# Gate products in float32 column quarters, in a kernel of attention, an MLP and a routed expert layer

## The chip, the cores and the metric

One core of one Trainium2 chip runs the whole program. The metric is the device time of one execution in microseconds. The engines are named as in the profile: PE is TensorE's matmul, PEld its weight load, DVE is VectorE, ACT is ScalarE, POOL is GpSimd, SP is SyncE, from whose queue nearly all DMAs are issued.

## The reference, cut to what matters

```python
# attention: q, k, v are 4 x 12 x 448 x 64; rows of q and k are normalized, softmax, product with v
x = attn.transpose(0, 2, 1, 3).reshape(1792, 768)
# MLP
h = x @ w_in                                # 768 x 2048
g = h * np.clip(h + 3.0, 0.0, 6.0) / 6.0
x = g @ w_out                               # 2048 x 768
# experts
logits = x @ w_gate                         # 768 x 8
# greedy assignment over all logits in falling order, at most 224 tokens per expert
# each token's expert: relu(x @ w1[e]) @ w2[e], 768 -> 1024 -> 768
```

The weights w_in and w_out may come as 64-bit floats, and the kernel first narrows them to float32.

## The kernel before, in words

A float32 product is made of three products in fp32r: each operand is split into a high part (a copy to fp32r, on ACT) and a low part (the rest, on DVE or POOL), and high x high, high x low and low x high are summed in PSUM. Some products with few columns (L371, L420 and L429 in the attention) are plain float32 products instead.

The program runs in this order. First the attention, two heads at a time, for four batches of 448 tokens. An order written out by hand (events with due times, and a queue of small pieces, "atoms", that `fill` draws from) sets every engine's order here. Between the attention of batch b the first MLP layer (L520) of batch b - 1 runs: for each of 16 units f of 128 hidden columns it does 18 products of 128 x 128 by 128 x 448, then ACT and DVE make g, and g goes to DRAM (g_dr). Then comes the first layer for batch 3, with nothing of the attention beside it. Then the second layer (L1135): 14 tiles of 128 tokens, by 16 f, by three products, by two column parts. The high and low parts g2h and g2l of g are read back from DRAM. Routing runs inside the second layer, a step after a given count of its products; it starts when the queue of leftover atoms is empty. The experts follow. From the first layer of batch 3 on only TensorE's order is written out; the other engines' orders, SP's DMA queue among them, come from a planner that lays them out by estimated times.

The logits are not taken from the second layer's result. They are computed as g @ (w_out @ w_gate), so that routing can run while the second layer does. Two parts serve that:

- `wprime_atoms` makes w_out @ w_gate in the attention of batch 3, merged into the first layer of batch 2. In 48 steps (8 pairs of units f, 6 chunks of 128 columns of w_out) it transposes two blocks (L659), splits the result into a high part (ACT, L661) and a low part (DVE, L662), and two steps later multiplies both with the gate's weights (L670, L671, L673; 8 or 16 stationary columns, 256 moving). The high and low products lie beside each other in 16 rows and are transposed back and added (L681 to L684); wp is the result, split again.
- `lg(b, f)` multiplies unit f of wp with unit f of g of batch b: two products of 448 columns (L570 and L571, or L573). `gsplit` makes the parts gh (ACT, L557) and gl (DVE, L558). For batch 3 this is done inline, two units behind the first layer. For batches 0 and 1, `late_lg_atoms` reads g back from DRAM into gr (L611, four buffers) and the atoms are merged into the first layer of batch 3. For batch 2 and the last two units of batch 3 the atoms are drawn from the queue in the second layer, one for every seven products. `lg_end` copies the 16 rows of a batch, transposes them in blocks of 128 tokens (L599) and adds high and low part into L, which routing reads.

In the first layer of batch 3 there also are the loads and splits of w_in (L178, L115, L116) and of w_out (L814, L115, L116).

Of the kernel before, what the change touches and what calls it, by code (L numbers as in the profile page):

```python
# [8 lines left out]
F32 = mybir.dt.float32  # L9
# [4 lines left out]
OP = mybir.AluOpType  # L14
# [7 lines left out]
def kernel(  # L22
# [82 lines left out]

    half = const.tile([128, 1], F32, name="half")
    nc.vector.memset(half, 0.5)
    wp = const.tile([128, NF, 16], F32R, name="wp")
    L = const.tile([128, NTC, E], F32, name="L")


# [382 lines left out]
    def mlp1_atoms(b, inline):  # L494
# [16 lines left out]
        def mm(f, n):  # L511
            if n == 0:
                unit_start(f)
            c, t = divmod(n, 3)
            wh, wl, w = state["w"]
            xh, xl = XT[b]
            lhs = (wh, wh, wl)[t]
            x = (xh, xl, xh)[t]
            p = state["ps"]
            nc.tensor.matmul(p[:, :S], lhs[:, c], x[:, c], start=(n == 0), stop=(n == 3 * NC - 1))  # L520
            if n == 3 * NC - 1:
                r = mpool.tile([128, S], F32, name="r", bufs=1)
                nc.scalar.activation(r, p[:, :S], AF.Relu, bias=half, scale=1.0 / 6.0)
                g = mpool.tile([128, S], F32, name="g", bufs=GB)
                nc.vector.scalar_tensor_tensor(g, r, 1.0, p[:, :S], op0=OP.min, op1=OP.mult)
                state["g", f] = g
                if inline:
                    gsplit(b, f, g, nc.vector)

        def g_out(f):  # L530
            nc.sync.dma_start(g_dr[b][f * 128:(f + 1) * 128, :], state.pop(("g", f)))
# [1 line left out]
        for f in range(NF):  # L533
            for n in range(3 * NC):
                atoms.append(lambda f=f, n=n: mm(f, n))
                if n == GD and f > 0:
                    atoms.append(lambda f=f: g_out(f - 1))
                if n == WD2 and b in whole_b:
                    atoms.append(prefetch)
                if inline and n == 10 and f > 1:  # L540
                    atoms.append(lambda f=f: lg(b, f - 2))
        atoms.append(lambda: g_out(NF - 1))
        if inline:
            for f in (NF - 2, NF - 1):
                late.append(lambda f=f: lg(b, f))
            late.append(lambda: lg_end(b, 0))
            late.append(lambda: lg_end(b, 1))
        return atoms
# [1 line left out]
    GS = {}  # L550
    LGM = {}

    def gsplit(b, f, g, eng):
        k, n = (1, GI) if b == B - 1 else (0, GL)
        gh = tpool[0].tile([128, S], F32R, name=f"gh{k}", bufs=n)
        gl = tpool[0].tile([128, S], F32R, name=f"gl{k}", bufs=n)
        nc.scalar.activation(gh, g, AF.Copy)  # L557
        eng.tensor_tensor(gl, g, gh.bitcast(F32), op=OP.subtract)  # L558
        GS[b, f] = (gh, gl)

    def lg(b, f):
        if f == 0:
            if b < B - 1:
                lgp[b] = ps.tile([128, 512], F32, name="lg", tag="b", bufs=8)
            else:
                lgp[b] = ps.tile([128, 512], F32, name="lg", tag="b", bufs=8)
        p = lgp[b]
        gh, gl = GS.pop((b, f))
        if f > 0:
            nc.tensor.matmul(p[:8, :S], wp[:, f, 0:8], gl, start=False, stop=False, skip_group_check=True)  # L570
        nc.tensor.matmul(p[:16, :S], wp[:, f, :], gh, start=(f == 0), stop=(f == NF - 1))  # L571
        if f == 0:
            nc.tensor.matmul(p[:8, :S], wp[:, f, 0:8], gl, start=False, stop=False, skip_group_check=True)  # L573

    def lg_end(b, part):

        p, odd = lgp[b], b % 2
        if part == 0:
            s = tpool[0].tile([16, S], F32, name="lgs", bufs=1)
            nc.vector.tensor_copy(s, p[:16, :S])  # L580
            if b // 2 not in LGM:
                LGM[b // 2] = [tpool[0].tile([16, 128], F32, name="lgm", bufs=2), 0]
            m = LGM[b // 2]
            m[1] += 1
            nc.scalar.activation(m[0][:, odd * 64:odd * 64 + 64], p[:16, 0:64] if odd else p[:16, S - 64:S], AF.Copy)
            lgp[b] = s
            return
        m, n = LGM[b // 2]
        s = p[:, odd * 64:odd * 64 + 384]
        src = [s[:, k * 128:(k + 1) * 128] for k in range(3)]  # L590
        c0 = 4 if odd else 0
        if n == 2:
            src = [m] + src if odd else src + [m]
# [2 lines left out]
        n = len(src)  # L596
        t = ps.tile([128, 512], F32, name="t", tag="b", bufs=8)
        for c, x in enumerate(src):
            nc.tensor.transpose(t[:, 16 * c:16 * c + 16], x, ident[:16, :16])  # L599
        s2 = tpool[0].tile([128, 4, 16], F32, name="lgs2", bufs=1)  # L600
        nc.scalar.activation(s2[:, :n], t[:, :16 * n].rearrange("p (c e) -> p c e", e=16), AF.Copy)
        c0 += 7 * (b // 2)
        nc.vector.tensor_tensor(L[:, c0:c0 + n, :], s2[:, :n, 0:8], s2[:, :n, 8:16], op=OP.add)

    def late_lg_atoms(bs):

        GR = {}

        def ld(b, f):
            GR[b, f] = tpool[0].tile([128, S], F32, name="gr", bufs=4)  # L610
            nc.sync.dma_start(GR[b, f], g_dr[b][f * 128:(f + 1) * 128, :])  # L611

        todo = [(b, f) for b in bs for f in range(NF)]
        atoms = []
        n = len(todo)
        for i in range(n + 4):
            def one(i=i):
                if i < n:
                    ld(*todo[i])
                if 1 < i < n + 2:  # L620
                    b, f = todo[i - 2]
                    gsplit(b, f, GR.pop((b, f)), nc.vector)
                if i > 3:
                    b, f = todo[i - 4]
                    if f == 1 and b != bs[0]:
                        lg_end(b - 1, 1)
                    lg(b, f)
                    if f == NF - 1:
                        lg_end(b, 0)
            atoms.append(one)  # L630
        atoms.append(lambda: lg_end(bs[-1], 1))
        return atoms


    def wprime_atoms():
        wg = apool.tile([128, NC, E], F32, name="wg", bufs=1)
        nc.sync.dma_start(wg, w_gate.rearrange("(c p) e -> p c e", p=128))
        wgs = apool.tile([128, NC, 16], F32R, name="wgs", bufs=1)
        nc.scalar.activation(wgs[:, :, 0:8], wg, AF.Copy)
        nc.vector.tensor_tensor(wgs[:, :, 8:16], wg, wgs[:, :, 0:8].bitcast(F32), op=OP.subtract)  # L640
        wsum = apool.tile([128, NF, E], F32, name="wsum", bufs=1)
        T3 = 3
        tt = apool.tile([128, T3, 2, 256], F32R, name="wo_t", bufs=1)
        raws, st = {}, {}

        def ld(f):
            raws[f] = stage("wo_v")
# [5 lines left out]
        def one(g, c):  # L653
# [6 lines left out]
            o = tt[:, (g * NC + c) % T3]  # L660
# [3 lines left out]
        def two(g, c):  # L664
            if c == 0:
                st["acc"] = ps.tile([128, 512], F32, name="lg", tag="b", bufs=8)
            p = st["acc"]
            o = tt[:, (g * NC + c) % T3]
            if c > 0:
                nc.tensor.matmul(p[:8, :256], wgs[:, c, 0:8], o[:, 1], start=False, stop=False, skip_group_check=True)  # L670
            nc.tensor.matmul(p[:16, :256], wgs[:, c], o[:, 0], start=(c == 0), stop=(c == NC - 1))  # L671
            if c == 0:
                nc.tensor.matmul(p[:8, :256], wgs[:, c, 0:8], o[:, 1], start=False, stop=False, skip_group_check=True)  # L673
            if c == NC - 1:
                st["s", g] = apool.tile([16, 256], F32, name="wps", bufs=2)
                nc.scalar.activation(st["s", g], p[:16, :256], AF.Copy)

        def three(g):
            t = ps.tile([128, 512], F32, name="h", tag="b", bufs=8)
            for k in range(2):  # L680
                nc.tensor.transpose(t[:, 16 * k:16 * k + 16], st["s", g][:, k * 128:(k + 1) * 128], ident[:16, :16])  # L681
            v = apool.tile([128, 2, 16], F32, name="wpv", bufs=2)
            nc.scalar.activation(v, t[:, :32].rearrange("p (f e) -> p f e", e=16), AF.Copy)
            nc.vector.tensor_tensor(wsum[:, 2 * g:2 * g + 2], v[:, :, 0:8], v[:, :, 8:16], op=OP.add)  # L684
            if g == NF // 2 - 1:
                nc.scalar.activation(wp[:, :, 0:8], wsum, AF.Copy)
                nc.vector.tensor_tensor(wp[:, :, 8:16], wsum, wp[:, :, 0:8].bitcast(F32), op=OP.subtract)

        todo = [(g, c) for g in range(NF // 2) for c in range(NC)]
        atoms = []  # L690
        for i in range(len(todo) + 4):
            def step(i=i):
                if i < len(todo):
                    one(*todo[i])
                if 1 < i < len(todo) + 2:
                    two(*todo[i - 2])
# [634 lines left out]
```

## Time and profile before

| | us |
|---|---|
| median of 3 runs | 1215.1 (1214.14 to 1218.32) |
| profiled execution | 1219.53 |
| its span | 1217.7 |
| TensorE busy | 1145.3 |
| VectorE busy | 780.7 |
| ScalarE busy | 552.1 |
| GpSimd busy | 490.6 |

The profile is of one execution. Its span runs from the first to the last instruction; all times in the rows below count from the span's start. Matmuls overlap in their pipeline, so the duration of one (0.36 us for 448 columns in fp32r) is longer than the distance from one start to the next. The mean granted TensorE clock is 0.978 of full speed.

### The profile page before, as it was taken

The numbers are of one execution on the slowest core, as the hardware profiler recorded it, in microseconds if no ns is written. First come the engines' busy times: TensorE is split into PE (matmuls) and PEld (weight loads), VectorE is DVE, ScalarE is ACT, GpSimd is POOL, SyncE is SP. The second block draws the span as 40 slices with busy tenths as digits, with TensorE's granted clock in tenths as the row PEclk, the third lists the DMA queues.
The fourth block names the chain that finished last, engine by engine and source line by source line (L and its number), as shares of the span: only waits on it lengthen the run. The fifth ranks groups of instructions, "written<-read, shape, count | busy, mean of one in ns | idle before, by whom it ended". The sixth has DMA issues, their size and how long they took to land.

```text
span 1217.7 us, 19761 instructions
## 1 busy us (share of the span) xinstructions
PE 1145.3 (94%) x7204; PEld 931.2 (76%) x7204; DVE 780.7 (64%) x1580; ACT 552.1 (45%) x1019; POOL 490.6 (40%) x362
## 2 busy tenths in 40 slices
PE   3988999999999999999979999999998799999997
PEld 2877656667676677787758787777778799999997
DVE  7887977767657665346893466666676675555550
ACT  3655646555454555446663111111123566555650
POOL 2222554754345432112352222222243677666640
PEclk9888999999999999999999999999999899999999
DMA  4355998977786866649895222222234688778731
GB/s 127 116 163 144 261 303 255 302 273 242 236 279 214 277 223 241 211 149 321 261 298 157 61 75 66 79 57 65 79 100 129 203 257 263 229 235 240 230 116 45
DMA packets 210708, 230.84 MB, mean 190 GB/s; under 512 B 24338, under 2 KB 183732, under 8 KB 210612
## 3 DMA queue, kind: packets, MB, share of 16 engines
q1 hardware_dynamic: 207284, 218.58, 58.3%
q0 software_dynamic: 3328, 11.01, 3.0%
q8 instruction: 56, 0.92, 0.3%
q14 instruction: 40, 0.33, 0.1%
HBM read 178.57 MB, written 50.98 MB: 189 GB/s over the span
## 4 chain that ended last, share of the span: by engine, by line
PE 62%; DVE 14%; DMA 9%; issue 6%; ACT 4%; POOL 2%; SPq 1%; POOLq 0%; DVEq 0%; ACTq 0%
PE y L1135 16%; PE h L520 10%; PE y L1283 8%; PE h L1219 5%; PE st L331 4%; PE av L420 3%; PE av L371 3%; PE h L1221 2%; PE sm L429 2%; PE rt L945 2%; DMA gr<-g_dr 1%; DMA wo_s<-wo 1%; PE s L309 1%; DVE C L940 1%; DMA we_s<-in_moe_w_dram 1%
## 5 line engine op out<-in xcount | busy, mean ns | idle before, releaser
L520 PE MATMUL h<-xh,w 128*128 128x448 f32 x768 | 240.3, 381 | 0.6 <-DVE mr L320 0.3
L520 PEld LDWEIGHTS h<-xh,w 128*128 128x128 f32 x768 | 144.8, 192 | 30.6 <-issue 14.3
L1078 POOL TENSOR_TENSOR g2l<-gr,g2h 128x512 fp32r<-128x512 f32 x60 | 79.1, 1319 | 207.1 <-ACT g2h L1076 159.8
L520 PE MATMUL h<-xl,w 128*128 128x448 f32 x384 | 145.7, 379 | 0.0
L312 DVE TENSOR_REDUCE mx<-s 112x1 f32<-112x448 f32 x192 | 105.9, 612 | 54.2 <-PE s L309 54.1
L1076 ACT ACTIVATE g2h<-gr 128x512 fp32r<-128x512 f32 x60 | 37.9, 631 | 207.1 <-PE y L1135 157.5
L1135 PE MATMUL y<-woh,g2l 128*128 128x512 f32 (+1 forms) x448 | 128.7, 349 | 1.0 <-POOL g2l L1078 1.0
L1135 PE MATMUL y<-woh,g2h 128*128 128x512 f32 (+1 forms) x448 | 128.1, 349 | 0.0
L1135 PE MATMUL y<-wol,g2h 128*128 128x512 f32 (+1 forms) x448 | 126.4, 346 | 0.0
L116 DVE TENSOR_TENSOR wel<-we_s,weh 128x768 fp32r<-128x768 f32 x59 | 80.6, 1372 | 61.5 <-ACT weh L115 59.2
L115 ACT ACTIVATE weh<-we_s 128x768 fp32r<-128x768 f32 x107 | 88.9, 842 | 59.3 <-DMA we_s<-in_moe_w_dram 41.1
L116 POOL TENSOR_TENSOR wel<-we_s,weh 128x768 fp32r<-128x768 f32 x48 | 95.5, 1991 | 46.7 <-ACT weh L115 36.0
L342 ACT ACTIVATE ph<-st 112x448 f32<-112x448 f32 x192 | 93.0, 544 | 46.9 <-PE st L331 46.0
L413 POOL TENSOR_TENSOR pa<-ph 112x448 f32<-112x448 f32 x68 | 85.8, 1282 | 53.6 <-ACT ph L342 53.4
L1219 PE MATMUL h<-xe,weh 128*128 128x448 f32 x318 | 101.4, 378 | 2.2 <-DVE xe L1170 2.2
L520 PEld LDWEIGHTS h<-xl,w 128*128 128x128 f32 x384 | 73.9, 192 | 10.8 <-issue 4.5
L1135 PEld LDWEIGHTS y<-woh,g2l 128*128 128x128 f32 x448 | 73.0, 190 | 10.9 <-POOL g2l L1078 1.3
L1135 PEld LDWEIGHTS y<-woh,g2h 128*128 128x128 f32 x448 | 73.0, 190 | 10.6 <-issue 1.4
L1135 PEld LDWEIGHTS y<-wol,g2h 128*128 128x128 f32 x448 | 72.6, 190 | 9.9 <-issue 0.2
L1221 PE MATMUL h<-xe,wel 128*128 128x224 f32 x318 | 77.2, 270 | 0.0
L1283 PE MATMUL y<-weh,hl 128*112 128x384 f32 x216 | 72.9, 338 | 0.0
L1283 PE MATMUL y<-weh,hh 128*112 128x384 f32 x216 | 72.8, 337 | 0.0
(256 smaller groups left out, 2493.4 us busy)
## 6 DMA issues: line engine op xcount, KB each, us to landing
we_s<-in_moe_w_dram SPq DMA_DIRECT2D x128, 384.0 KB
w<-w_hl SPq DMA_DIRECT2D x32, 768.0 KB
g_dr<-g SPq DMA_DIRECT2D x64, 224.0 KB
gr<-g_dr SPq DMA_DIRECT2D x52, 256.0 KB
wraw<-in_moe_w_in_dram SPq DMA_DIRECT2D x16, 768.0 KB
win_v<-w SPq DMA_DIRECT2D x32, 384.0 KB
w_hl<-w SPq DMA_DIRECT2D x16, 768.0 KB
wraw<-in_moe_w_out_dram SPq DMA_DIRECT2D x16, 768.0 KB
```

Of the source, the lines that this page charges most:

```text
L115: nc.scalar.activation(hi, raw, AF.Copy)
L116: eng.tensor_tensor(lo, raw, hi.bitcast(F32), op=OP.subtract)
L312: mx = nc.vector.tensor_reduce(MX[i][:, s, c:c + 1], pp[s][:CP, :S], axis=AX.X, op=OP.max)
L331: nc.tensor.matmul(pp[s][:CP, :S], a[r], b[r], start=(n == 0), stop=(n == len(todo) - 1))
L342: nc.scalar.activation(e, pp[s][:CP, :S], AF.Exp)
L413: nc.gpsimd.tensor_tensor(PA[i, s, n], PP[i, s, 2 * n][0], PP[i, s, 2 * n + 1][0], op=OP.add)
L520: nc.tensor.matmul(p[:, :S], lhs[:, c], x[:, c], start=(n == 0), stop=(n == 3 * NC - 1))
L1078: eng.tensor_tensor(gl, g, gh.bitcast(F32), op=OP.subtract)
L1135: nc.tensor.matmul(pp[hf][:, :COLS[hf].stop - COLS[hf].start], a[:, f % QF], w[:, COLS[hf]], start=(f == 0 and n == 0), stop=(f == NF - 1 ...
L1219: mm = [lambda: nc.tensor.matmul(p[:, :4 * CP], wh[:, fo], x.rearrange("d k t -> d (k t)"), start=(c == 0), stop=(c == NC - 1), skip_group ...
L1221: lambda: nc.tensor.matmul(p[:, :2 * CP], wl[:, fo], x[:, 0], start=False, stop=False, skip_group_check=True)]
L1283: nc.tensor.matmul(p[:CP, :HW], a[:, f, tk], w[:, o], start=(f == 0 and n == 0), stop=(f == FB - 1 and n == 2))
```

## The change

Both gate products become plain float32 products, and the splits around them go.

In `wprime_atoms` the transposed blocks are only copied (ACT); six of them are multiplied together at the end of a pair of units, each against 32 stationary columns of the gate's weights of which the first 8 count (the others are neighbours' or zero padding), and written to one of three quarters of 32 rows of PSUM. One reduction on DVE then sums the three quarters after the transposes back.

In `lg` a burst does four units f at once, each with 32 stationary columns of wp (again 8 that count) into its own quarter of 32 rows. `gsplit` goes; g of batch 3 is kept in six buffers, gr has eight buffers, and a burst follows two groups of four loads behind. `lg_end` copies 128 rows instead of 16 (ACT), keeps the 64 columns at the seam between batches with DVE, transposes blocks of 128 x 128, and one reduction on DVE sums the quarters.

```diff
+    QW, WQ = 32, 3
+    wp = const.tile([128, NF + 3, E], F32, name="wp")
+    nc.vector.memset(wp, 0.0)
...
                 if inline:
-                    gsplit(b, f, g, nc.vector)
+                    GS[b, f] = g
...
-                if inline and n == 10 and f > 1:
-                    atoms.append(lambda f=f: lg(b, f - 2))
+                if inline and n == 10 and f > 4 and f % LQ == 1:
+                    atoms.append(lambda f=f: lg(b, f // LQ - 1))
...
-        gh, gl = GS.pop((b, f))
-        if f > 0:
-            nc.tensor.matmul(p[:8, :S], wp[:, f, 0:8], gl, start=False, stop=False, skip_group_check=True)
-        nc.tensor.matmul(p[:16, :S], wp[:, f, :], gh, start=(f == 0), stop=(f == NF - 1))
...
+        for u in range(LQ):
+            f = fq * LQ + u
+            nc.tensor.matmul(p[u * QW:(u + 1) * QW, :S], wp[:, f:f + QW // E].rearrange("p f e -> p (f e)"), GS.pop((b, f)), start=(fq == 0), stop=(fq == NF // LQ - 1))
...
-            nc.vector.tensor_copy(s, p[:16, :S])
+            nc.scalar.activation(s, p[:, :S], AF.Copy)
...
+            nc.tensor.transpose(t[:, 128 * c:128 * c + 128], x, ident)
...
+        nc.vector.tensor_reduce(L[:, c0:c0 + n, :], t[:, :128 * n].rearrange("p (c u x) -> p c x u", u=LQ, x=QW)[:, :, 0:8, :],
+                                axis=AX.X, op=OP.add)
...
+            GS[b, f] = tpool[0].tile([128, S], F32, name="gr", bufs=2 * LQ)
...
+                    if u == 0 and k > 1:
+                        burst(*todo[k - 2])
+                    if k < len(todo):
+                        ld(todo[k][0], todo[k][1] * LQ + u)
...
-            nc.scalar.activation(o[:, 0], t[:, :256], AF.Copy)
-            nc.vector.tensor_tensor(o[:, 1], t[:, :256], o[:, 0].bitcast(F32), op=OP.subtract)
+            tt[g, c] = apool.tile([128, 256], F32, name="wo_t", bufs=TB)
+            nc.scalar.activation(tt[g, c], t[:, :256], AF.Copy)
...
+        def two(g):
+            p = ps.tile([128, 512], F32, name="lg", tag="b", bufs=8)
+            for c in range(NC):
+                r = c % WQ * QW
+                nc.tensor.matmul(p[r:r + QW, :256], wg[:, c:c + QW // E].rearrange("p c e -> p (c e)"), tt.pop((g, c)),
+                                 start=(c < WQ), stop=(c >= NC - WQ))
```

## Rows read from the trace of the kernel before

**Rows 1.** The page: shares of the chain that ended last, by engine.

```profile
PE 62%; DVE 14%; DMA 9%; issue 6%; ACT 4%; POOL 2%; SPq 1%; POOLq 0%; DVEq 0%; ACTq 0%
```

**Rows 2.** By windows: stretch, its length, busy us per engine (instructions), clock, DMA.

```profile
541.60:635.90 94.30, 82.82 (x390) 65.05 (x389) 74.73 (x86) 61.21 (x107) 36.58 (x19) 0.96 0.92 283
635.90:644.70 8.80, 8.80 (x37) 6.79 (x36) 5.71 (x20) 2.15 (x5) 3.72 (x8) 0.67 0.78 244
...
422.00:541.60 119.60, 119.21 (x762) 91.97 (x758) 57.53 (x117) 59.55 (x137) 30.51 (x26) 1.00 0.64 214
644.70:682.00 37.30, 37.30 (x210) 30.24 (x210) 14.94 (x33) 13.18 (x25) 9.36 (x8) 1.00 0.41 116
```

**Rows 3.** Timeline of PE: start, us, operation, and idle time before it with releaser.

```profile
548.14 0.38 PE L571 MATMUL lg<-gh,wp 128*16 128x448 f32 x1 [2.31 <-ACT gh L557]
...
603.85 0.37 PE L570 MATMUL lg<-gl,wp 128*8 128x448 f32 x1 [2.22 <-DVE gl L558]
...
619.51 0.37 PE L570 MATMUL lg<-gl,wp 128*8 128x448 f32 x1 [3.13 <-DVE gl L558]
...
635.33 0.28 PE L599 MATMUL t<-ident,lgm 16*128 16x16 f32 x1 [3.21 <-ACT lgm L585]
```

**Rows 4.** Groups of instructions from 541.6 to 635.9: busy us, mean ns, idle before.

```profile
L558 DVE TENSOR_TENSOR gl<-gr,gh 128x448 fp32r<-128x448 f32 x35 | 34.9, 1006 | 9.5 <-ACT gh L557 9.5
...
L571 PE MATMUL lg<-gh,wp 128*16 128x448 f32 x46 | 17.0, 372 | 2.3 <-ACT gh L557 2.3
...
L558 DVE TENSOR_TENSOR gl<-g,gh 128x448 fp32r<-128x448 f32 x15 | 14.7, 983 | 1.4 <-ACT gh L557 1.2
```

**Rows 5.** Waits of SP's queue, same stretch: us in total, times, longest.

```profile
SPq L611 <- DVE gl L558: 20.4, 18, 3.6
```

**Rows 6.** DMA in the same stretch: all packets, and one group of issues.

```profile
DMA packets 26461, 26.64 MB, mean 283 GB/s; under 512 B 1443, under 2 KB 24406, under 8 KB 26454
...
we_s<-in_moe_w_dram SPq DMA_DIRECT2D x6, 384.0 KB
```

**Rows 7.** By windows, 5 us in the middle of the stretch.

```profile
565.00:570.00 5.00, 5.00 (x26) 4.02 (x25) 4.22 (x6) 3.33 (x7) 1.99 (x2) 1.00 1.13 337
```

**Rows 8.** The chain in order of time: start, us, what.

```profile
547.75 6.43 DMA gr<-g_dr
```

**Rows 9.** Timeline of PE around logit products in the first layer.

```profile
597.79 0.36 PE L571 MATMUL lg<-gh,wp 128*16 128x448 f32 x1
...
599.61 0.58 PE L520 MATMUL h<-xh,w 128*128 128x448 f32 x2
```

**Rows 10.** Products in column halves: timeline at 129.49, at 264.8; the chain's sm.

```profile
129.49 0.60 PE L420 MATMUL av<-ph,vv 112*64 112x448 f32 x2
...
264.81 0.37 PE L520 MATMUL h<-xh,w 128*128 128x448 f32 x1
265.10 3.23 PE L420 MATMUL av<-ph,vv 112*64 112x448 f32 x16
268.16 1.67 PE L429 MATMUL sm<-pa,ones 112*64 112x448 f32 x8
269.76 0.47 PE L520 MATMUL h<-xh,w 128*128 128x448 f32 x1
270.07 0.36 PE L520 MATMUL h<-xl,w 128*128 128x448 f32 x1
...
268.33 1.50 PE sm L429 x8
```

**Rows 11.** Timeline of PE in one step of wprime; the transposes as a group.

```profile
434.73 0.38 PE L659 MATMUL h<-ident,wo_v 128*128 128x128 f32 x2
434.86 0.36 PE L670 MATMUL lg<-wo_t,wgs 128*8 128x256 f32 x1
435.06 0.28 PE L671 MATMUL lg<-wo_t,wgs 128*16 128x256 f32 x1
435.18 0.37 PE L520 MATMUL h<-xh,w 128*128 128x448 f32 x1
...
L659 PE MATMUL h<-ident,wo_v 128*128 128x128 f32 x96 | 18.4, 273 | 0.0
```

More of the change, by code (lines that the diff above doesn't have):

```diff
@@ L107 @@
     nc.vector.memset(half, 0.5)
-    wp = const.tile([128, NF, 16], F32R, name="wp")
+    QW, WQ = 32, 3
+    wp = const.tile([128, NF + 3, E], F32, name="wp")
+    nc.vector.memset(wp, 0.0)
     L = const.tile([128, NTC, E], F32, name="L")
@@ L523, in mm @@
                 nc.scalar.activation(r, p[:, :S], AF.Relu, bias=half, scale=1.0 / 6.0)
-                g = mpool.tile([128, S], F32, name="g", bufs=GB)
+                g = tpool[0].tile([128, S], F32, name="gi", bufs=6) if inline else mpool.tile([128, S], F32, name="g", bufs=GB)
                 nc.vector.scalar_tensor_tensor(g, r, 1.0, p[:, :S], op0=OP.min, op1=OP.mult)
@@ L539, in mlp1_atoms @@
                     atoms.append(prefetch)
-                if inline and n == 10 and f > 1:
-                    atoms.append(lambda f=f: lg(b, f - 2))
+                if inline and n == 10 and f > 4 and f % LQ == 1:
+                    atoms.append(lambda f=f: lg(b, f // LQ - 1))
         atoms.append(lambda: g_out(NF - 1))
         if inline:
-            for f in (NF - 2, NF - 1):
-                late.append(lambda f=f: lg(b, f))
+            late.append(lambda: lg(b, NF // LQ - 1))
             late.append(lambda: lg_end(b, 0))
@@ L551, with lg @@
     LGM = {}
[L553 to L566, printed above, removed]
-        p = lgp[b]
-        gh, gl = GS.pop((b, f))
-        if f > 0:
-            nc.tensor.matmul(p[:8, :S], wp[:, f, 0:8], gl, start=False, stop=False, skip_group_check=True)
-        nc.tensor.matmul(p[:16, :S], wp[:, f, :], gh, start=(f == 0), stop=(f == NF - 1))
-        if f == 0:
-            nc.tensor.matmul(p[:8, :S], wp[:, f, 0:8], gl, start=False, stop=False, skip_group_check=True)
+    LQ = 4
+    QP = (LQ - 1) * QW + 8
+    def lg(b, fq):
+        if fq == 0:
+            lgp[b] = ps.tile([128, 512], F32, name="lg", tag="b", bufs=8)
+        p = lgp[b]
+        for u in range(LQ):
+            f = fq * LQ + u
+            nc.tensor.matmul(p[u * QW:(u + 1) * QW, :S], wp[:, f:f + QW // E].rearrange("p f e -> p (f e)"), GS.pop((b, f)), start=(fq == 0), stop=(fq == NF // LQ - 1))
     def lg_end(b, part):
@@ L578, in lg_end @@
         if part == 0:
-            s = tpool[0].tile([16, S], F32, name="lgs", bufs=1)
-            nc.vector.tensor_copy(s, p[:16, :S])
+            s = tpool[0].tile([128, S], F32, name="lgs", bufs=1)
+            nc.scalar.activation(s, p[:, :S], AF.Copy)
             if b // 2 not in LGM:
-                LGM[b // 2] = [tpool[0].tile([16, 128], F32, name="lgm", bufs=2), 0]
+                LGM[b // 2] = [tpool[0].tile([128, 128], F32, name="lgm", bufs=1), 0]
             m = LGM[b // 2]
             m[1] += 1
-            nc.scalar.activation(m[0][:, odd * 64:odd * 64 + 64], p[:16, 0:64] if odd else p[:16, S - 64:S], AF.Copy)
+            nc.vector.tensor_copy(m[0][:, odd * 64:odd * 64 + 64], p[:, 0:64] if odd else p[:, S - 64:S])
             lgp[b] = s
@@ L589, in lg_end @@
         s = p[:, odd * 64:odd * 64 + 384]
-        src = [s[:, k * 128:(k + 1) * 128] for k in range(3)]
+        src = [s[:, c * 128:(c + 1) * 128] for c in range(3)]
         c0 = 4 if odd else 0
@@ L598, in lg_end, with burst, one @@
         for c, x in enumerate(src):
-            nc.tensor.transpose(t[:, 16 * c:16 * c + 16], x, ident[:16, :16])
-        s2 = tpool[0].tile([128, 4, 16], F32, name="lgs2", bufs=1)
-        nc.scalar.activation(s2[:, :n], t[:, :16 * n].rearrange("p (c e) -> p c e", e=16), AF.Copy)
+            nc.tensor.transpose(t[:, 128 * c:128 * c + 128], x, ident)
         c0 += 7 * (b // 2)
-        nc.vector.tensor_tensor(L[:, c0:c0 + n, :], s2[:, :n, 0:8], s2[:, :n, 8:16], op=OP.add)
+        nc.vector.tensor_reduce(L[:, c0:c0 + n, :], t[:, :128 * n].rearrange("p (c u x) -> p c x u", u=LQ, x=QW)[:, :, 0:8, :],
+                                axis=AX.X, op=OP.add)
     def late_lg_atoms(bs):
-        GR = {}
         def ld(b, f):
-            GR[b, f] = tpool[0].tile([128, S], F32, name="gr", bufs=4)
-            nc.sync.dma_start(GR[b, f], g_dr[b][f * 128:(f + 1) * 128, :])
-        todo = [(b, f) for b in bs for f in range(NF)]
-        atoms = []
[L615 to L630, printed above, removed]
+            GS[b, f] = tpool[0].tile([128, S], F32, name="gr", bufs=2 * LQ)
+            nc.sync.dma_start(GS[b, f], g_dr[b][f * 128:(f + 1) * 128, :])
+        todo = [(b, fq) for b in bs for fq in range(NF // LQ)]
+        def burst(b, fq):
+            if fq == 1 and b != bs[0]:
+                lg_end(b - 1, 1)
+            lg(b, fq)
+            if fq == NF // LQ - 1:
+                lg_end(b, 0)
+        atoms = []
+        for k in range(len(todo) + 1):
+            for u in range(LQ):
+                def one(k=k, u=u):
+                    if u == 0 and k > 1:
+                        burst(*todo[k - 2])
+                    if k < len(todo):
+                        ld(todo[k][0], todo[k][1] * LQ + u)
+                atoms.append(one)
+        atoms.append(lambda: burst(*todo[-1]))
         atoms.append(lambda: lg_end(bs[-1], 1))
@@ L635, in wprime_atoms @@
     def wprime_atoms():
[L636 to L644, printed above, removed]
+        wg = apool.tile([128, NC + 3, E], F32, name="wg", bufs=1)
+        nc.gpsimd.memset(wg[:, NC:], 0.0)
+        nc.sync.dma_start(wg[:, :NC], w_gate.rearrange("(c p) e -> p c e", p=128))
+        TB = 8
+        raws, st, tt = {}, {}, {}
         def ld(f):
@@ L659, in one @@
                 nc.tensor.transpose(t[:, k * 128:(k + 1) * 128], raws[2 * g + k][:, c * 128:(c + 1) * 128], ident)
-            o = tt[:, (g * NC + c) % T3]
-            nc.scalar.activation(o[:, 0], t[:, :256], AF.Copy)
-            nc.vector.tensor_tensor(o[:, 1], t[:, :256], o[:, 0].bitcast(F32), op=OP.subtract)
[L664 to L676, printed above, removed]
+            tt[g, c] = apool.tile([128, 256], F32, name="wo_t", bufs=TB)
@@ new lines, in one @@
+            nc.scalar.activation(tt[g, c], t[:, :256], AF.Copy)
[5 more added lines that the diff above has]
+                                 start=(c < WQ), stop=(c >= NC - WQ))
+            st[g] = apool.tile([WQ * QW, 256], F32, name="wps", bufs=2)
+            nc.scalar.activation(st[g], p[:WQ * QW, :256], AF.Copy)
@@ L678, in three @@
         def three(g):
             t = ps.tile([128, 512], F32, name="h", tag="b", bufs=8)
+            s = st.pop(g)
             for k in range(2):
[L681 to L684, printed above, removed]
@@ L685, in three @@
-            if g == NF // 2 - 1:
-                nc.scalar.activation(wp[:, :, 0:8], wsum, AF.Copy)
-                nc.vector.tensor_tensor(wp[:, :, 8:16], wsum, wp[:, :, 0:8].bitcast(F32), op=OP.subtract)
+                nc.tensor.transpose(t[:, k * WQ * QW:(k + 1) * WQ * QW], s[:, k * 128:(k + 1) * 128], ident[:WQ * QW, :WQ * QW])
+            nc.vector.tensor_reduce(wp[:, 2 * g:2 * g + 2, :],
+                                    t[:, :2 * WQ * QW].rearrange("p (f u x) -> p f x u", u=WQ, x=QW)[:, :, 0:E, :],
+                                    axis=AX.X, op=OP.add)
@@ L694, in step @@
                     one(*todo[i])
-                if 1 < i < len(todo) + 2:
-                    two(*todo[i - 2])
+                if i > 1 and i - 2 < len(todo) and todo[i - 2][1] == NC - 1:
+                    two(todo[i - 2][0])
                 if i > 3 and todo[i - 4][1] == NC - 1:
```

## The prediction, made before the changed kernel was run

> **What bounds the kernel now.** The page first: TensorE holds 62% of the chain that ended last, VectorE 14% [rows 1]. So time is saved where TensorE works without pause, by giving it less, and where it pauses, by removing what it waits for. The two products that change lie in three stretches, which the view by windows separates [rows 2]. From 422 to 541.6 us (attention of batch 3 with the product of w_out and the gate) TensorE is busy 119.2 of 119.6 us: this stretch is bound by TensorE. From 541.6 to 635.9 us (first layer for batch 3, gate logits of batches 0, 1 and 3, the split of w_out) it is busy 82.8 of 94.3, VectorE 74.7, and the DMA engines have a share of 0.92. From 644.7 us on (second layer with the logits of batch 2) TensorE is again never idle. Between the last two lie 8.8 us in which its granted clock is 0.67: that is a mean over 2.4 GHz and 1.2 GHz, after a pause.
>
> The timeline of TensorE shows the pauses of the middle stretch: 2.31, 2.22, 3.13 and 3.21 us [rows 3], 10.9 of its 11.5 us. Two end on VectorE's subtraction gl, one on ScalarE's gh, one on the copy lgm. The groups of instructions say why: gl is run 50 times there, 49.6 us of VectorE's 74.7, at a mean of 1006 and 983 ns [rows 4], and SyncE's queue waits 20.4 us for gl before it may load the next gr into its buffer [rows 5]. So part of the DMA traffic, too, is held back by VectorE. For each f, TensorE then does two logit products that cost as much as any other.
>
> **The change, part by part.**
>
> *One product of 448 columns in fp32r.* Between 597.79 and 599.61 us TensorE starts nine of them, one lg, six h and an lg pair (the first and the row after the last are shown): 1.82 / 9 = 0.202 us each, for lg as for h [rows 9]. A pair for one f costs 0.40, four f cost 1.62 us.
>
> *Four fp32 products in column quarters.* The trace has no quarters, but it has halves: av (L420) and sm (L429) are float32 products of 448 columns, put into two 64-column halves. The narrow view at 129.49 us shows two passes in flight at once. Each product has two passes: 8 products of av make 16 rows, 4 of sm make 8. The chain has eight passes of sm in 1.50 us: four steps of two, 0.375 a step. The way in and out costs more: 0.29 us from the last h to the first av instead of 0.20 (0.09); from 265.10 to 269.76 us the 24 passes take 4.66 instead of 12 x 0.375 = 4.50 (0.16); and the first h behind them is followed after 0.31 instead of 0.20 (0.11): 0.36 together [rows 10]. If four quarters run at once as two halves do, a burst of four f is 2 steps x 0.375 + 0.36 = 1.11 us instead of 1.62. This is the term whose size is unknown: if only two run at once it is 4 x 0.375 + 0.36 = 1.86, if none, 8 x 0.375 + 0.36 = 3.36. I take 1.11, since halves reach the full factor of two in the nearest rows.
>
> The Trainium skill ("TensorE: Matmul & The Clock Gate", Part 3: Packing small matmuls) speaks against the full factor: it gives 2.38 for three column tiles and 3.07 for four row tiles. By those figures the burst would be an estimated 3.0 / 3.07 + 0.36 = 1.34 us and the forecast some 3 us less gain; no row here shows more than two tiles side by side.
>
> *Product of w_out and the gate's weights (wprime).* Now 48 steps; one runs from 434.73 to 435.18 us: 0.45, of which the two transposes are 0.22 (the pair takes 0.38, one alone 0.27, so they start 0.11 apart) [rows 11]. The two fp32r products thus cost 0.23 x 48 = 11.0 us. After: 8 bursts of six products of 256 columns in three quarters, two rounds of two passes: 4 x 0.375 x 256/448 + 0.36 = 1.22 us, 9.8 us in all. **-1.2 us**, on the path since TensorE is never idle there. Bounds: -4.1 (if the way in and out is nothing behind float32 transposes, 8 x 0.36 less) and +12.4 (no overlap: 12 x 0.214 + 0.36 = 2.93 a burst). VectorE loses 48 subtractions and gains 8 small reductions in place of 8 adds; ScalarE keeps its copies. Both are about half busy in that window [rows 2], so neither counts. The memsets of wp and wg are a few hundred columns on VectorE while the first loads are on their way and on POOL at 25% load: 0.
>
> *The middle stretch.* TensorE's own work after: 288 h x 0.202 = 58.2, 11 bursts (8 of batches 0 and 1, 3 of batch 3) x 1.11 = 12.2, seven transposes x 0.11 = 0.8: 71.2 us instead of 94.3. VectorE falls from 74.7 to about 25 us, ScalarE loses the 50 gh, so what ends three of the four pauses is gone: gr goes from DMA straight into TensorE. The fourth (lgm) keeps its chain, now ScalarE's copy of all 128 rows and VectorE's of 64 columns, but no subtraction stands ahead of it, and nine h products (1.8 us) lie between. What is late next is DMA: 26.64 MB moved in the stretch [rows 6], and 5 us at its fullest moved 337 GB/s [rows 7]: 79 us for all of it; without the six loads of we_s (2.36 MB, not needed before the experts) 72. A wait is added: gr has eight buffers, and the first load of a group now waits for the burst two groups earlier on TensorE itself. Behind it on SyncE's queue stand the loads of w_in and w_out. SyncE waits 20.4 us there today for gl; the load-to-use distance is 5 to 8 atoms of the merged list, each about 9 products or 1.8 us, so 9 to 16 us against the 6.43 us that a gr load takes in the chain [rows 8]. I take this wait as covered; uncovered it is the first rival. Between 71.2 (TensorE alone) and 94.3 (as now) I take 79, the traffic at full rate: **-15.3 us**.
>
> *The start of the second layer.* The 8.8 us at clock 0.67 lose about 2.9; I count nothing, with -2.9 as the lower bound, for some pause at the seam stays likely.
>
> *Second layer.* Of the 64 pairs 46 (of L571) were done before 635.9 [rows 4], so 18 pairs, 36 x 0.202 = 7.3 us, become 5 bursts = 5.5: **-1.8 us** (bounds -3.6, if the way in and out is nothing, and +9.5 without overlap). The list keeps its 25 pieces (4 + 21 before, 3 + 22 after) and so routing, which starts when it is empty, starts at the same product of the second layer; everything behind moves with it.
>
> Sum: -1.2 - 15.3 - 1.8 = -18.3. Against the profiled execution (1219.5 us: span 1217.7 and 1.8 around it) that is 1201; the median of the runs is 1215.1, 4.4 lower, and I put the gain there: about 1197 us.
>
> **Rivals.**
>
> *DMA takes the place of VectorE.* For: a share of 0.92 over the stretch already, with SyncE held back. Against: 337 GB/s is possible, and much of the traffic is wanted only later. If the stretch falls only to 87, because loads of gr or w_in come late and each wait also halves the clock for a while, the gain is 1.2 + 7.3 + 1.8 = 10: 1205.
>
> *Only two quarters at once.* Stretch: 59.0 + 11 x 1.86 = 79.5, with the waits between that and DMA's 79 some 83: -11; second layer 5 x 1.86 - 7.3 = +2; wprime with rounds of two and one, 8 x (8 x 0.214 + 0.36) = 16.6 - 11.0 = +5.6. Together -3.4: 1212.
>
> *Quarters don't overlap (slower).* Stretch: 59.0 + 11 x 3.36 = 96.0, +1.7; second layer 16.8 - 7.3 = +9.5; wprime 23.4 - 11.0 = +12.4. Together +24: 1239. It decides where a burst of four costs b = 2.3 us or more: 59.0 + 11b - 94.3, 5b - 7.3 and about 8 x 0.86b - 10.6 add to nought there; that is an overlap under 1.5-fold. Against it stand the halves, fully side by side; for it, that a quarter moves four streams at once and no row shows that.
>
> *All smooth.* Stretch at 71.2 + 2 (-21.1), the start at full clock (-2.9), the rest as forecast (-3.0): -27: 1188.
>
> **How the numbers follow.** Forecast (stretch 76 to 82) 0.45, DMA 0.22, all smooth 0.15, two quarters 0.09, no overlap 0.05, another planned order of loads in the stretch that costs about what is gained 0.04. Predicted 1197. A range from 1186 to 1211 leaves out most of the last three and a little at the low end, under 2 in 10. 0.3% is 3.6 us, about what can be told from no change here: faster (under 1211.5) 0.88, within 0.04, slower 0.08.
>
> **What would show it.** Passes of lg starting four within some 20 ns and the next four 0.37 us later; a burst near 1.1 us from h to h. No row of gl or gh. In the stretch TensorE's pauses under 5 us in all, VectorE about 25 us, DMA above 300 GB/s and the stretch near 79 us. wprime's window shorter by 1 to 3 us. Routing starting about as far behind the first y product as before. I am wrong if passes come in twos or ones, or if TensorE's pauses before lg name DMA gr and add up to more than 10 us.

## The result, and the profile after

The changed kernel takes 1187.2 us (median of 4 runs, 1185.3 to 1188.9) against 1215.0 for the kernel before (1214.1 to 1218.3); the ratio is 0.9766, 95% interval 0.9743 to 0.979. That is 27.7 us less where 18.3 were forecast: inside the range, 1.2 us from its edge, and at the time given for the rival "all smooth" (1188). One run of an experiment below, 1521.9 us at a granted clock of 0.66, was in a slower state than all others and isn't counted.

The page after, shares of the chain that ended last:

```profile
PE 67%; DVE 13%; DMA 8%; issue 5%; ACT 3%; POOL 3%; SPq 1%; POOLq 0%; DVEq 0%; ACTq 0%
```

By windows, the same four stretches as in [rows 2], at their new times (length; busy us of PE, PEld, DVE, ACT, POOL; clock, DMA share, GB/s):

```profile
424.90:534.50 109.60, 109.20 (x732) 81.70 (x730) 37.07 (x63) 55.59 (x123) 27.27 (x23) 1.00 0.67 220
534.50:607.25 72.75, 71.91 (x387) 55.76 (x385) 23.82 (x33) 32.43 (x47) 26.64 (x17) 1.00 1.01 330
607.25:616.00 8.75, 7.17 (x41) 4.82 (x40) 5.82 (x21) 3.19 (x6) 2.52 (x6) 1.00 0.92 312
616.00:654.20 38.20, 38.20 (x228) 29.95 (x228) 7.39 (x23) 10.01 (x16) 18.10 (x12) 1.00 0.62 185
```

The middle stretch went from 94.3 to 72.75 us. VectorE has 23.8 us there instead of 74.7, the clock is 1.00 instead of 0.96 (and 1.00 instead of 0.67 behind it), and TensorE is idle for 0.84 us instead of 11.5. DMA is at a share of 1.01, which reads like a limit and, as the experiments below show, is not one yet.

The timeline of TensorE around one burst, the same product by product (start, us, operation); the first row is a view of 30 ns:

```profile
554.71 0.58 PE L564 MATMUL lg<-gr,wp 128*32 128x448 f32 x4
...
554.21 0.57 PE L522 MATMUL h<-xh,w 128*128 128x448 f32 x2
554.71 0.96 PE L564 MATMUL lg<-gr,wp 128*32 128x448 f32 x8
555.60 0.47 PE L522 MATMUL h<-xl,w 128*128 128x448 f32 x1
555.91 0.57 PE L522 MATMUL h<-xh,w 128*128 128x448 f32 x2
```

Four passes start within 30 ns. From the first of the eight passes to the h behind them it is 0.89 us (554.71 to 555.60). With 0.09 to get in (from the h at 554.41, 0.30 instead of 0.20) and 0.11 behind (0.31 instead of 0.20) that is 1.09: the forecast had 1.11.

What is left of the pauses at lg, in the stretch and just behind it, with the rest of each burst and the product that follows:

```profile
544.97 0.95 PE L564 MATMUL lg<-gr,wp 128*32 128x448 f32 x6
546.76 0.94 PE L564 MATMUL lg<-gr,wp 128*32 128x448 f32 x2 [0.84 <-DMA gr<-g_dr]
547.63 0.47 PE L522 MATMUL h<-xh,w 128*128 128x448 f32 x1
...
608.71 0.95 PE L564 MATMUL lg<-gi,wp 128*32 128x448 f32 x6
611.24 0.94 PE L564 MATMUL lg<-gi,wp 128*32 128x448 f32 x2 [1.58 <-DVE gi L527]
612.11 0.38 PE L1112 MATMUL y<-woh,g2h 128*128 128x256 f32 x1
```

A pause inside a burst costs more than the idle time beside it, since the last product then runs alone: these two bursts take 2.66 and 3.40 us instead of 0.89, so they lose 1.8 and 2.5 us.

And the DMA of the stretch, to be read against [rows 6]; the six loads of we_s are no longer in it:

```profile
DMA packets 22362, 23.98 MB, mean 330 GB/s; under 512 B 1341, under 2 KB 20565, under 8 KB 22355
```

By stage, between the same instructions of both profiles: up to the first transpose of wprime 427.1 to 424.9 (-2.1); from there to the first h of batch 3 114.6 to 109.5 (-5.1); to the first y product 94.2 to 72.8 (-21.4); to the first product of routing 49.2 to 46.9 (-2.2); the rest 532.7 to 531.6 (-1.2). Together -32, since the profiled execution of before lay 4.6 us above its median and that of the changed kernel 0.3. The first and the last item hold none of the changed products, and they are what varies between executions: the changed kernel, profiled a second time, reached the first transpose at 421.3 us and took 2.0 us longer in the last item, while the three items between differed by 0.2, 0.1 and 0.04 us. So the stages are compared below, each beside the total.

### The profile page after: what moved, and what is told of

It reads as the page before. It is cut to its first block, busy times and chain, and to the rows that moved or that the text cites. A ratio compares the mean times of both kernels' runs of the same rounds, so it can differ in the third digit from the quotient of the medians.

```text
span 1185.7 us, 19464 instructions
## 1 busy us (share of the span) xinstructions
PE 1121.4 (95%) x7204; PEld 907.1 (76%) x7204; DVE 704.5 (59%) x1467; ACT 520.7 (44%) x941; POOL 486.7 (41%) x363
## 4 chain that ended last, share of the span: by engine, by line
PE 67%; DVE 13%; DMA 8%; issue 5%; ACT 3%; POOL 3%; SPq 1%; POOLq 0%; DVEq 0%; ACTq 0%
PE y L1112 17%; PE h L522 15%; PE y L1260 8%; PE h L1196 5%; PE st L333 4%; PE av L422 3%; PE h L1198 3%; PE av L373 2%; PE sm L431 2%; DMA w<-cv 2%; PE rt L922 2%; DMA we_s<-in_moe_w_dram 1%; DVE C L917 1%; DMA w_hl<-w 1%; PE lg L564 1%
## 5 line engine op out<-in xcount | busy, mean ns | idle before, releaser
L1112 PEld LDWEIGHTS y<-woh,g2h 128*128 128x128 f32 x448 | 71.9, 189 | 11.7 <-issue 2.3
L525 ACT ACTIVATE r<-h,half 128x448 f32<-128x448 f32 x64 | 40.7, 635 | 74.3 <-PE h L522 61.4
```

Of the source, the lines that this page charges most:

```text
L1112: nc.tensor.matmul(pp[hf][:, :COLS[hf].stop - COLS[hf].start], a[:, f % QF], w[:, COLS[hf]], start=(f == 0 and n == 0), stop=(f == NF - 1 ...
```

## The experiments

Each edit is to the changed kernel unless said otherwise. "Stretch" is from the first h of batch 3 to the first y product.

**Do the quarters overlap, and what sets the stretch?** All four products of a burst in one quarter, and on two:

```diff
-            nc.tensor.matmul(p[u * QW:(u + 1) * QW, :S], wp[:, f:f + QW // E]..., GS.pop((b, f)), start=(fq == 0), stop=(fq == NF // LQ - 1))
+            v = u % 1        # u % 2, u < 2 and LQ - 2 in the second kernel
+            nc.tensor.matmul(p[v * QW:(v + 1) * QW, :S], wp[:, f:f + QW // E]..., GS.pop((b, f)),
+                             start=(fq == 0 and u < 1), stop=(fq == NF // LQ - 1 and u >= LQ - 1))
```

> The changed kernel with all four products of a logit burst in the same quarter of 32 columns, so that none can run beside another; 32 rows are copied and transposed at the end. Theory A (the quarters really run side by side, and TensorE's own work sets the stretch of the first layer of batch 3 now): a burst goes from 0.89 to 8 x 0.375 = 3.0 us, less a little for the way in and out; 16 bursts, +32 to +36 us: 1219 to 1223, slower than the kernel before although VectorE is as free as in the changed kernel. Theory B (the gain comes from VectorE's relief and DMA sets the stretch at its share of 1.01, so TensorE has room): the 11 bursts of that stretch are largely hidden, +10 to +15 us: 1197 to 1202.

> The changed kernel with the four products of a logit burst on two quarters (first and third on one, second and fourth on the other); 64 rows are copied and transposed at the end. Theory A: a burst takes 4 x 0.375 = 1.5 + 0.14 instead of 0.89, 16 x 0.75 = +12 us: 1199. Theory B (DMA sets the stretch): only the five bursts outside it count, +4 us: 1191.

Measured: one quarter 1219.1 us, ratio to the kernel before 1.0028 (1.0006 to 1.005); two quarters 1196.9, 0.9846 (0.9817 to 0.9876). Windows of the stretch and the timeline at a burst, one quarter:

```profile
534.15:629.84 95.69, 95.69 (x386) 62.41 (x384) 29.41 (x37) 37.33 (x53) 34.74 (x22) 1.00 0.90 283
```

```profile
561.41 3.19 PE L565 MATMUL lg<-gi,wp 128*32 128x448 f32 x8
564.53 0.68 PE L522 MATMUL h<-xh,w 128*128 128x448 f32 x2
```

The same of two quarters:

```profile
535.60:615.22 79.62, 79.62 (x387) 57.96 (x385) 30.55 (x37) 36.87 (x52) 31.19 (x20) 1.00 1.00 325
```

```profile
560.26 1.70 PE L565 MATMUL lg<-gi,wp 128*32 128x448 f32 x8
561.89 0.67 PE L522 MATMUL h<-xh,w 128*128 128x448 f32 x2
```

A burst takes 3.12, 1.63 and 0.89 us with one, two and four quarters, and the stretch 95.7, 79.6 and 72.8. In the first two the profile has no idle time of TensorE. That is theory A. The prediction's rivals "quarters don't overlap" and "only two quarters" had TensorE's own work there at 96.0 and 79.5. So without the overlap of lg the change gains nothing, though it frees VectorE nearly as much (29.4 us of it in the stretch, 23.8 in the changed kernel and 74.7 in the kernel before). From four to two quarters the stretch grows by 6.9 where the bursts grow by 11 x 0.74 = 8.1; the first burst's wait for gr, 1.8 us in the changed kernel and 0.4 with two quarters, is what lies between.

**Is DMA that limit?** The first try copied g once more, from DRAM to DRAM, beside each load of gr:

```diff
             nc.sync.dma_start(GS[b, f], g_dr[b][f * 128:(f + 1) * 128, :])
+            if b < LB:
+                nc.sync.dma_start(g_x[b][f * 128:(f + 1) * 128, :], g_dr[b][f * 128:(f + 1) * 128, :])
```

> The changed kernel with, beside each of the 32 loads of g of batches 0 and 1, a copy of the same 224 KB from DRAM to DRAM that nobody waits for: 7.3 MB read and written more. Theory A (TensorE sets the stretch, loads have slack): under 5 us more, 1187 to 1192. Theory B (DMA at its share of 1.01 sets it): 7.3 MB at 330 to 380 GB/s are at least 19 us, 1206 or more.

Measured: 1200.0 us, 0.9851 (0.982 to 0.9882), between the two theories. The view of the tile says why it tells nothing of the stretch (first and last start are the last two numbers):

```profile
L602 SPq DMA_DIRECT2D g_x<-g_dr x32: 473/496/1547, 160.2 to 423.2; - x32
```

The planner issued all 32 copies between 160 and 423 us, in the attention. The stretch stayed at 72.6 us; from the first h of batch 0 to the first h of batch 3 it is 14.4 us longer. So the second try wrote each gr out again from its buffer, which can't happen earlier:

```diff
                     if k < len(todo):
                         ld(todo[k][0], todo[k][1] * LQ + u)
+                    if 0 < k <= len(todo) and todo[k - 1][0] < LB:
+                        b, f = todo[k - 1][0], todo[k - 1][1] * LQ + u
+                        nc.sync.dma_start(g_x[b][f * 128:(f + 1) * 128, :], GS[b, f])
```

> The changed kernel with each gr of batches 0 and 1 written out again to DRAM after its load, 32 x 224 KB that nobody waits for but its own buffer: 7.3 MB more that must move within the stretch, which the copies from DRAM to DRAM did not do. TensorE sets the stretch and its loads have slack: 72.8 stays under 76. DMA sets it: 24 + 7.3 = 31.3 MB at 330 to 380 GB/s are 82 to 95 us.

Measured: 1194.9 us (median of three runs), 0.9838 (0.9813 to 0.9863). Windows and DMA of the stretch:

```profile
534.22:618.19 83.97, 78.03 (x386) 56.69 (x385) 24.50 (x34) 33.93 (x48) 28.22 (x17) 1.00 1.03 356
```

```profile
DMA packets 26060, 29.90 MB, mean 356 GB/s; under 512 B 1750, under 2 KB 24241, under 8 KB 26053
```

The stretch grew by 11.2 us with 5.9 MB more, to 84.0, which is what "DMA sets it" had expected. TensorE's groups there say where (shapes; count; busy us, mean ns of one; idle before them, and what ended it), first the changed kernel, then this one:

```profile
L522 PE MATMUL h<-xh,w 128*128 128x448 f32 x193 | 56.6, 369 | 0.0
L564 PE MATMUL lg<-gr,wp 128*32 128x448 f32 x64 | 8.6, 551 | 0.8 <-DMA gr<-g_dr 0.8
```

```profile
L523 PE MATMUL h<-xh,w 128*128 128x448 f32 x193 | 56.8, 370 | 0.0
L565 PE MATMUL lg<-gr,wp 128*32 128x448 f32 x64 | 14.7, 551 | 5.9 <-DMA gr<-g_dr 5.9
```

The products h are as before; all of it is at lg: 5.1 us more idle before the bursts, ended by loads of gr, and 6.1 more inside them, between their first and their last product. So with more to move the loads come late and DMA sets the stretch; whether by its rate or by the order of the issues in SyncE's queue, this run doesn't tell apart. In slices of 14 us it moved up to this much:

```profile
548.00:562.00 14.00, 14.00 (x77) 11.11 (x76) 3.93 (x6) 4.93 (x8) 1.84 (x1) 1.00 1.09 369
604.00:618.19 14.19, 13.07 (x62) 8.54 (x61) 4.93 (x8) 6.92 (x10) 5.59 (x4) 1.00 1.04 393
```

At 369 GB/s the changed kernel's 23.98 MB need 65 us, and at this run's mean of 356 it is 67: there DMA isn't the limit, though it is only some 5 us from it, and TensorE, busy for 71.9 of 72.75 us, is. The Trainium skill ("Perfetto Trace Analysis", Roofline) counts 358 GB/s as a core's share of HBM when both cores of a pair use it, and puts the practical ceiling of a core that runs alone at some 120% of it; 393 is 110%, which agrees.

**Which engine's work made the pauses?** One operation per tile of g put back where gl, gh or both had been, in place, between load and product; in one kernel into a scratch tile in bf16, so that VectorE has the work but TensorE doesn't wait for it:

```diff
+    def touch(x):
+        nc.vector.tensor_tensor(x, x, x, op=OP.max)                  # dve_chain
+        nc.scalar.activation(x, x, AF.Copy)                          # act_chain; both_chain: this, then the line above
+        o = tpool[0].tile([128, S], BF16, name="scr", bufs=1)        # dve_load: this line and the next
+        nc.vector.tensor_tensor(o, x, x, op=OP.max)
...
                 if inline:
+                    touch(g)
                     GS[b, f] = g
...
+                    if 0 < k <= len(todo):
+                        touch(GS[todo[k - 1][0], todo[k - 1][1] * LQ + u])
```

> The changed kernel with one operation of VectorE put back for each of the 64 tiles of g: x = max(x, x), in place, between the load (or the making) of g and the product, where gl was. ScalarE's gh stays away, the products stay as changed. Theory A (VectorE's 50 us in the stretch were what made the pauses): VectorE rises from 24 to some 60 to 75 us of the stretch, pauses before lg and half clocks come back, +6 to +15 us: 1193 to 1202. Theory C (the pauses came from ScalarE's copy and from the two engines in a row, VectorE alone keeps up): within 2 us of 1187.

> As the chain experiment, but VectorE writes max(x, x) to a scratch tile that nobody reads: the same load on VectorE and the same hold on the buffers of g, while TensorE does not wait for it. Theory A1 (the queue of loads and VectorE's other work, g and the splits, suffer from the load itself): nearly as long as the chain experiment, 1192 to 1200. Theory A2 (only TensorE's wait on VectorE cost time): 1187 to 1189.

> The changed kernel with one copy by ScalarE put back for each of the 64 tiles of g, in place, between its load (or making) and the product, where gh was; nothing on VectorE. If ScalarE's 50 copies (28 us in the stretch) are a cause beside VectorE's subtractions, the stretch grows from 72.8 to some 76 to 80 us, as with VectorE's operation alone (80.4): 1191 to 1195. If only VectorE mattered: within 1 us of 72.8.

> The changed kernel with both put back for each tile of g: ScalarE's copy in place, then VectorE's max in place, then the product. Theory D (the stretch's 21.4 us are TensorE's products, 18.6 - 12 = 6.6, and for the rest the chain through two busy engines): the stretch comes to 94.2 - 6.6 = 87.6, so 86 to 89 us, total about 1202. Theory E (each engine's load acts by itself, the sum of the two single experiments): what VectorE's operation alone added, 7.6, and what ScalarE's copy alone adds.

Measured, with the window of the stretch of each. VectorE in the chain, 1194.2 us, 0.9811 (0.9777 to 0.9846):

```profile
532.71:613.07 80.36, 73.87 (x386) 56.69 (x385) 68.87 (x93) 33.90 (x49) 32.36 (x21) 0.97 0.96 310
```

VectorE beside the chain, 1192.5 us, 0.9813 (0.9772 to 0.9854):

```profile
534.81:612.64 77.83, 73.97 (x387) 56.89 (x385) 67.68 (x86) 32.51 (x47) 31.80 (x20) 0.98 0.96 308
```

ScalarE in the chain, 1185.2 us, 0.9757 (0.9736 to 0.9779):

```profile
534.19:608.58 74.39, 72.13 (x386) 55.71 (x385) 25.23 (x41) 56.56 (x98) 27.48 (x20) 1.00 1.01 326
```

Both in the chain, 1194.2 us, 0.9833 (0.9806 to 0.986):

```profile
534.04:613.34 79.30, 73.31 (x386) 56.32 (x385) 65.69 (x94) 57.29 (x99) 31.21 (x21) 0.99 0.98 315
```

VectorE's work puts 7.6 us back into the stretch, 5.1 of them even where nothing waits for its result. ScalarE's adds 1.6 alone, between its two expectations, and nothing beside VectorE's. Beside the chain VectorE's work costs TensorE a longer pause elsewhere, before an h whose weights VectorE splits in the same queue:

```profile
605.58 0.99 PE L522 MATMUL h<-xh,w 128*128 128x448 f32 x2 [2.04 <-DVE w L118]
```

Theories A1 and A hold in kind; theories D (87.6) and E (7.6 + 1.6 more, 82.0) both fell, with 79.3 measured. With VectorE in the chain the longest pause is the last, at the end of the stretch, and it waits for a small copy that stands in VectorE's queue behind the tiles of g:

```profile
612.31 0.47 PE L594 MATMUL t<-ident,lgm 128*128 128x128 f32 x1 [3.96 <-DVE lgm L580]
```

The first burst takes 5.1 us there instead of 2.66, and the other ten take 0.89 as in the changed kernel. So VectorE's load costs time at the two ends of the stretch, not at every burst.

That leaves some 7 us of the stretch's 21.4 that neither TensorE's products (6.6, below) nor these operations account for. What the kernel before had besides is four buffers for gr instead of eight, loads two steps before the split and products two steps behind it, one f at a time. None of that was put back; the share of each is open.

**The two parts apart.** First the changed kernel with the old wprime, whose sums now go straight into wp; then the kernel before with the new one, its result split at its end as before. Of each edit the line that makes the sums:

```diff
-            nc.vector.tensor_reduce(wp[:, 2 * g:2 * g + 2, :],                                          # lg_only
...
+            nc.vector.tensor_tensor(wp[:, 2 * g:2 * g + 2], v[:, :, 0:8], v[:, :, 8:16], op=OP.add)
...
-            nc.vector.tensor_tensor(wsum[:, 2 * g:2 * g + 2, :], v[:, :, 0:8], v[:, :, 8:16], op=OP.add)  # wprime_only
...
+            nc.vector.tensor_reduce(wsum[:, 2 * g:2 * g + 2, :],
...
             if g == NF // 2 - 1:
                 nc.scalar.activation(wp[:, :, 0:8], wsum, AF.Copy)
```

> The changed kernel with the product of w_out and the gate as in the kernel before (high and low parts in fp32r, added to float32 at the end); logits as changed. Theory A (that product's part is worth what the two traces show between its first and last instruction, 109.5 against 114.5 us): 4 to 5 us come back, 1191 to 1192. The prediction's own term (1.2 us from one step's row): 1188.5.

> The kernel before with the product of w_out and the gate as changed (float32, three quarters), its result split again; logits as before. Theory A: 4 to 5 us less than before, 1210 to 1211. The prediction's term: 1213.8. If the two parts do not add up (this gain and the other single change's against 27.7), one of them makes room for the other.

Measured: 1192.9 us, 0.9817 (0.9785 to 0.9849), and 1213.3 us, 0.9978 (0.9957 to 1.0). The first total is near theory A, the second near the prediction's term; they are too wide to tell 4 us apart, and the windows of wprime are not. The logits alone:

```profile
424.06:538.42 114.36, 113.93 (x732) 87.67 (x730) 54.49 (x111) 55.97 (x130) 26.61 (x23) 1.00 0.64 212
```

wprime alone, and the stretch behind it:

```profile
423.66:533.20 109.54, 109.25 (x731) 81.98 (x730) 36.44 (x63) 55.58 (x123) 26.66 (x23) 1.00 0.68 220
533.20:630.65 97.45, 84.46 (x391) 65.42 (x389) 71.69 (x91) 60.84 (x106) 36.48 (x24) 0.94 0.90 276
```

In its own window wprime is worth 4.8 to 5.1 us wherever it stands, and the stretch belongs to the logits: 71.8 us with them alone, 97.5 without. But with wprime alone the stretch is also 3.2 us longer than in the kernel before (94.2), which takes most of its gain: 2.3 us are left in the total, with an interval that ends at nothing. Why it is longer isn't traced. So the logits' part doesn't need the other; that wprime's 5 us reach the total without the logits isn't shown.

**The pause behind the stretch.** The last burst of batch 3 and its end three pieces later in the list:

```diff
-    queue += late + (late_lg_atoms(range(LB, B - 1)) if LB < B - 1 else [])
+    lla = late_lg_atoms(range(LB, B - 1))
+    queue += lla[:3] + late + lla[3:]
```

> The changed kernel with the last burst of batch 3 and its end three pieces later in the list that the second layer draws from (three loads of batch 2 go first). The pause of 1.58 us before that burst, which waits for the last g, should go: 1185.6, if nothing waits in its place; 1187 if the pause only moves.

Measured: 1184.7 us, 0.9755 (0.9729 to 0.978). From the first y product to the first of routing, where it was 46.9:

```profile
606.80:651.25 44.45, 44.45 (x267) 34.63 (x265) 13.63 (x44) 13.16 (x21) 20.70 (x18) 1.00 0.72 221
```

TensorE has no idle time left there, and the burst takes 0.89 us instead of 3.40: that is the 2.5 us. In the totals it can't be told from the changed kernel.

**The changed kernel again**, beside the last three:

> The changed kernel itself, beside the three above on the same chip: 1187, stretch 72.8; how far its stages differ from its first profile is the measure for the stages of the others.

1188.6 us, 0.9799 (0.9774 to 0.9824); stretch 72.9. Two sets of runs of one kernel thus give 0.9766 and 0.9799: differences of 0.3% between totals of different sets are not read as effects here.

## Why the prediction was right, and where its sizes were off

The mechanism was right: the quarters overlap, and VectorE's work had held the stretch back (put back, it costs 7.6 us). That the total is near "all smooth" (1188, given 0.15) is in part luck. Its stretch came as it says (-21.1 and -21.4), but wprime gained 3.9 us more than it had, and the start and the second layer 2.5 less. Against the forecast, both large terms were mis-sized the same way, and so the time lies near the edge of the range.

*The burst.* 1.11 forecast, 1.09 measured, the overlap as in the halves: the step that carried the sign held. The price of its failure, 1239, was tested for lg alone, with wprime left overlapping (1219): of its terms, +1.7 in the stretch came as +1.5, and +9.5 in the second layer as +6.7 (from the first y product to the first of routing, 49.2 to 55.9); +12.4 for wprime was not tried. The Trainium skill ("TensorE: Matmul & The Clock Gate", Part 3: Packing small matmuls) gives a gain of 2.38 for three column tiles and 3.07 for four row tiles. Here four column tiles gain 3.12 / 0.89 = 3.5, so the measurement is above both.

*The middle stretch* (-15.3 forecast, -21.4 measured). The mis-sized term is "I take 79, the traffic at full rate". DMA did not become the limit: it had 23.98 MB to move, not 26.64, since loads for the experts, which the prediction had named as not needed (its own sum without them was 72), moved behind the stretch, and it can move more than the 337 GB/s taken (369 and 393 above). So the stretch fell to TensorE's own work, 71.2 forecast and 71.9 measured. A sum for it: lg products 92 x 0.202 = 18.6 to 11 x 1.09 = 12.0 (-6.6); pauses 11.5 to 0.84 (-10.7); the remaining 4 are mostly the half clock, 0.96 to 1.00 over the stretch. The prediction's DMA rival lets each wait halve the clock for a while, and that isn't so. In the kernel before, the windows around the first and the second pause of [rows 3] have a mean clock between half and full; behind the third, the longest but one, it is full:

```profile
545.00:555.00 10.00, 7.29 (x29) 5.38 (x28) 4.20 (x8) 4.36 (x9) 0.00 (x0) 0.83 0.94 275
600.00:610.00 10.00, 7.78 (x31) 6.00 (x31) 9.56 (x11) 7.28 (x13) 3.63 (x2) 0.83 0.77 229
619.00:629.00 10.00, 9.49 (x47) 7.67 (x48) 9.73 (x12) 7.60 (x13) 3.83 (x2) 1.00 0.96 312
```

The wait that the change adds, loads of gr behind bursts, was covered, as forecast, but for the first burst (1.8 us).

*The product of w_out and the gate* (-1.2 forecast, -5.1 measured). The bursts cost 1.19 each (1.22 forecast). Mis-sized was the old part, taken from one step in the middle of a pair. At the end of each of the 8 pairs two transposes of 16 rows followed, with a way in and out of their own; the timeline of the kernel before:

```profile
451.46 0.28 PE L671 MATMUL lg<-wo_t,wgs 128*16 128x256 f32 x1
451.67 0.29 PE L681 MATMUL h<-ident,wps 16*128 16x16 f32 x2
451.89 0.47 PE L520 MATMUL h<-xl,w 128*128 128x448 f32 x1
452.20 0.55 PE L286 MATMUL t<-ident,xn 112*128 112x112 f32 x4
```

From L671 to L681 0.21 us instead of 0.12, 0.22 for the two, and 0.31 instead of 0.20 for the h behind: 0.42 each. In the changed kernel the two transposes have 96 rows and follow the other transposes directly; a step with them and one without:

```profile
447.79 0.38 PE L644 MATMUL h<-ident,wo_v 128*128 128x128 f32 x2
448.00 0.33 PE L661 MATMUL h<-ident,wps 96*128 96x96 f32 x2
448.12 0.45 PE L522 MATMUL h<-xl,w 128*128 128x448 f32 x1
448.40 0.55 PE L288 MATMUL t<-ident,xn 112*128 112x112 f32 x4
...
449.62 0.38 PE L644 MATMUL h<-ident,wo_v 128*128 128x128 f32 x2
449.76 0.45 PE L522 MATMUL h<-xh,w 128*128 128x448 f32 x1
450.05 0.37 PE L522 MATMUL h<-xl,w 128*128 128x448 f32 x1
```

From the first transpose to the second instruction behind the transposes it is 0.61 us with the pair and 0.43 without: some 0.2 for the pair, so 8 x 0.22 = 1.8 more. With 0.2 from the bursts that makes 3.2 of the 5.1. Another 0.7 lies in the attention: with the old wprime three of eight pairs of products s (L309) start 0.2 us apart, with the new one each pair within 20 ns; "logits alone" and "wprime alone" show the same. The last 1.2 isn't traced.

*The start and the second layer* (0 and -1.8 forecast, -2.2 together). The full clock came (-2.9) and so did the shorter bursts (-1.8), but one new wait took 2.5 us back: the last burst of batch 3 waits for the last g, seven products into the second layer. The prediction had seen a pause at the seam as likely, without its place.

## What to carry to other kernels

Where a product has only eight columns of weights, as here, plain float32 products side by side in column quarters can cost TensorE less than products of split parts (1.09 against 1.62 us for four f), and the splits go. Price the queues of the engines that split, not only the products: here a third of the stretch's gain came from products, the rest went with pauses that ended on VectorE or ScalarE and with the half clock behind most of them, and the experiments gave back about half of that rest. When DMA is taken as the next limit, count only the bytes that the stretch must move, and check the rival by adding bytes that can't leave the stretch.

## What the runs showed of the hardware that was not expected

Float32 products in four column quarters run side by side: eight passes of 448 columns in 0.89 us against 3.12 in one quarter. A pair of transposes of 16 rows between fp32r products costs 0.42 us; a pair of 96 rows behind other float32 transposes some 0.2. An engine's load can cost nearly as much beside a chain as in it: VectorE's scratch operations, for which TensorE never waited, took 5.1 us where those in the chain took 7.6; the longest of the pauses, 2.0 us, waited for other work in VectorE's queue. And DMA moved 393 GB/s over 14 us with the clock at 1.00 beside it.
